# Gated linear attention and a mixture of experts on one core: first unit in halves, rows ahead of weights, verdict in the last expert, the angle's carry placed later

## The chip, the cores and the metric

The kernel runs on one core of one Trainium2 chip. The metric is the device time of one execution in microseconds (us), lower is better. A core has a matrix engine (TensorE, PE in the profile; PEld are its weight loads), three engines for elementwise work (VectorE or DVE, ScalarE or ACT, GpSimd or POOL), and SyncE (SP), which here issues most of the transfers between device memory and on-chip memory. Each engine runs its own list of instructions in order, and waits on semaphores for what others produce. A layer above the kernel's code decides in which order the instructions of one engine stand, so the order of the Python lines is only a wish.

## What is computed

Two blocks follow each other. The first is a linear attention with a complex gate: for each of 4 batches and 8 heads a 48x48 complex state is carried over 768 time steps.

```python
mag = np.sqrt(a_re * a_re + a_im * a_im)
scale = np.minimum(mag, 0.999) / (mag + 1e-06)
a_re_n, a_im_n = (a_re * scale, a_im * scale)
for t in range(S):
    new_re = ar * S_re - ai * S_im
    new_im = ar * S_im + ai * S_re
    kv = np.einsum('bhd,bhe->bhde', k[:, :, t], v[:, :, t])
    S_re, S_im = (new_re + kv, new_im)
    y[:, :, t] = np.einsum('bhd,bhde->bhe', q[:, :, t], S_re)
```

Its output, 3072 rows of 384 numbers, goes into the second block: each row chooses one of 8 experts by the largest of 8 logits, and the expert is two matrix products.

```python
expert_idx = np.argmax(logits, axis=1)
...
h = np.maximum(x_sorted[lo:hi] @ w1[e], 0.0)   # w1[e]: 384 x 1024
y_sorted[lo:hi] = h @ w2[e]                    # w2[e]: 1024 x 384
...
return gate_w[:, None] * y
```

## The kernel before

The attention is computed in chunks of 128 time steps. A *unit* is one such chunk of two batches, a tile of 128 x 768 numbers for each input (128 x 384 a batch); there are 12. The gate is turned into a logarithm of its size, `A`, and an angle, `ai`; both are summed along time by products with triangular matrices (`csl` and `cst`). The chain for a unit alternates between ScalarE and VectorE:

```python
def decay_steps(u):
    ar, ai = T["ar", u], T["ai", u]
    ...
    def s0():
        act(out=A, in_=ar, func=AF.Ln)
    def s1():
        act(out=R, in_=A, func=AF.Exp, scale=-1.0)
        nc.vector.tensor_tensor(out=ai, in0=ai, in1=R, op=OP.mult)
        act(out=R, in_=ai, func=AF.Square)
    def s2():
        act(out=R, in_=R, func=AF.Ln, bias=1.0)
        nc.vector.scalar_tensor_tensor(out=A, in0=A, scalar=2.0, in1=R, ...)
    def s3():
        act(out=R, in_=A, func=AF.Exp, scale=-0.5, bias=ln2e6)
        nc.vector.scalar_tensor_tensor(out=A, in0=A, scalar=LN_CAP2, in1=R, ...)
    return [s0, s1, s2, s3]
```

The angle then goes through an arctangent. From unit 2 on it also needs the angle that the same batches had reached at the end of the chunk before (`fl`); this is the *carry*. The last row is taken out of the tile by a small transfer, added to on VectorE, and put back by another:

```python
def decay_angle(u):
    act(out=th, in_=th, func=AF.Arctan)
    if u * U >= B:
        nc.gpsimd.dma_start(out=T["c0", u], in_=th[0:1]...)      # "c<-ai" in the profile

def carry_angle(u):
    if u * U >= B:
        nc.vector.scalar_tensor_tensor(out=c0, in0=T["fl", u - B // U], ..., in1=c0, ...)
        nc.gpsimd.dma_start(out=T["th", u][0:1]..., in_=c0)      # "ai<-c"
```

Sines and cosines of the summed angle (`CS`) turn the scaled queries and keys (`Q`, `K`), which TensorE transposes (`tp`); copies `qt` and `kt` of the transposed tiles feed the products `at`, and so on to the output `y`. The program starts with the loads, with matmuls on an identity matrix that serve no result (`busy`, tile `idle`; they keep TensorE at work), and with unit 0's chain. In the loop, unit u's sums stand beside unit u+1's chain:

```python
load_a(0)          # ar, ai of unit 0
load_qkv(0)
...                # the gate weights wg
load_a(1)
busy(None, 30)
table("natural_log_exp_and_others")
for f in decay_steps(0):
    f()
...
for u in range(NU + 1):
    ...
        steps = decay_steps(u + 1) if u + 1 < NU else []
        own = [lambda c=c: decay_sums(u, c) for c in range(U)]
        steps = steps[:1] + (own + steps[1:] if u == 0 else own[:1] + steps[1:2] + own[1:] + steps[2:])
        for i, f in enumerate(steps):
            f()
            if i == 1:
                carry_angle(u)
```

After the attention, rows have been scattered to memory in the order of their experts (`xs`). An expert's rows are gathered (`sq`, and `gi` for gate and index), transposed on VectorE (`xt`, function `turn`), multiplied by w1 (`hps`), cut at zero (`ht`), multiplied by w2 (`yps`), scaled by the gate (`y`) and scattered to the output. Expert 0 comes in two parts. Weights have two buffers, rows have two, and SyncE issues all these loads in order.

```python
rest0 = gather(0, FIRST, tiles(CAPS[0] - FIRST))
experts_at(range(1, E), False)
load_w(1)
...
parts = [(0, [P] * (FIRST // P), own0), (0, tiles(CAPS[0] - FIRST), rest0)]
xt = turn(parts[0][1], own0[0])
for e in range(E):
    while parts and parts[0][0] == e:
        sizes, (sq, gi) = parts.pop(0)[1:]
        if not parts and e + 1 < E:
            parts.append((e + 1, tiles(CAPS[e + 1]), gather(e + 1, 0, tiles(CAPS[e + 1]))))
        ...
        def ahead():                   # called between hps and yps
            if parts:
                T["xt"] = turn(parts[0][1], parts[0][2][0])
        expert(sizes, xt, *W_T[e], gi, todo, ahead)
        xt = T["xt"]
    if e + 2 < E:
        load_w(e + 2)
    ...
    if e == E - 2:
        verdict()
```

Beside experts 1 to 6, ScalarE and GpSimd check that the inputs lie in the range for which the fast attention is valid. `verdict` gathers these checks into a flag by a few VectorE operations and one tiny matmul (`bp`); at the very end of the program the flag decides whether a slow attention has to run instead, which does not happen with these inputs.

Of the kernel before, what the change touches and what calls it, by code (L numbers as in the profile page):

```python
# [10 lines left out]
FP = mybir.dt.float32  # L11
# [3 lines left out]
OP = mybir.AluOpType  # L15
# [5 lines left out]
P = 128  # L21
# [16 lines left out]
def kernel(  # L38
# [189 lines left out]
    def act(**kw):  # L228

        ins = nc.scalar.activation(**kw)  # L230
        if "act" in T:
            queue(ins, T["act"])
        T["act"] = ins
# [20 lines left out]
                queue(w, m)  # L254
            m = w

    def load(u, names):
        for nm, src in names:
            if nm == "v":
                t = vbuf[u % 3][:, :, :, 0:D]  # L260
                T[nm, u] = vbuf[u % 3]
            else:
                t = ld.tile([P, U, H, D], FP, tag=nm, name=nm, bufs=3 if nm == "ai" else 2)
                T[nm, u] = t.rearrange("p c h d -> p (c h d)")
            s, b = divmod(u * U, B)
            T["ld"] = nc.sync.dma_start(
                out=t.rearrange("p c h d -> p (c h) d"),
                in_=src[b : b + U, :, s * P : (s + 1) * P, :].rearrange("b h t d -> t (b h) d"),
            )

    def load_a(u):
        load(u, (("ar", a_re), ("ai", a_im)))
# [1 line left out]
    def load_qkv(u):  # L274
        load(u, (("q", q), ("k", k), ("v", v)))

    def decay_steps(u):

        ar, ai = T["ar", u], T["ai", u]
        A = un.tile([P, W], FP, tag="A", name="A")  # L280
        R = un.tile([P, W], FP, tag="R", name="R", bufs=1)
        T["L", u], T["th", u] = A, ai

        def s0():
            act(out=A, in_=ar, func=AF.Ln)

        def s1():
            act(out=R, in_=A, func=AF.Exp, scale=-1.0)
            nc.vector.tensor_tensor(out=ai, in0=ai, in1=R, op=OP.mult)
            act(out=R, in_=ai, func=AF.Square)  # L290

        def s2():
            act(out=R, in_=R, func=AF.Ln, bias=1.0)
            nc.vector.scalar_tensor_tensor(out=A, in0=A, scalar=2.0, in1=R, op0=OP.mult, op1=OP.add)

        def s3():

            act(out=R, in_=A, func=AF.Exp, scale=-0.5, bias=ln2e6)
            nc.vector.scalar_tensor_tensor(out=A, in0=A, scalar=LN_CAP2, in1=R, op0=OP.min, op1=OP.subtract)

        return [s0, s1, s2, s3]

    def decay_angle(u):

# [51 lines left out]
    def angle_sums(u, c):  # L356

        if c == 0:
            for nm in ("f", "fa"):
                T[nm, u] = un.tile([P, W], FP, tag=nm, name=nm, bufs=1)  # L360
        sl = slice(c * DM, (c + 1) * DM)
        f = T["f", u][:, sl]
        cs = sums("cst", u, c)
        m = mm(cs, tri_turn, T["th", u][:, sl])
        if u == 0 and c == 1:
            busy(m, 28)
        r = ch.tile([P, DM], FP, tag="r", name="r")
# [182 lines left out]
    def gather(e, s, sizes):  # L550

        n, w = len(sizes), sum(sizes)
        f, nb = w // P, -(-w // TB)
        sq = gp.tile([P, nb, KD * TB], FP, tag="sq", padded_shape=[P, CAP // TB, KD * TB], name="sq")
        gi = gp.tile([P, n, 2], FP, tag="gi", padded_shape=[P, CT, 2], name="gi", bufs=3)
        rows = xs[0:NS].rearrange("(e s) c -> e s c", s=CAP)[ds(ex[e], 1), s : s + nb * TB]
        for a in range(QB):  # L560
            x = rows[:, :, a * KD * TB : (a + 1) * KD * TB]
            nc.sync.dma_start(out=sq[a * TB : (a + 1) * TB], in_=x.rearrange("o (b j) c -> j (o b) c", j=TB))
        nc.sync.dma_start(out=gi[:, :f], in_=rows[:, : f * P, DM:].rearrange("o (i p) c -> p (o i) c", p=P))
        if f < n:
            nc.sync.dma_start(out=gi[0 : w - f * P, f], in_=rows[:, f * P : w, DM:].rearrange("o p c -> (o p) c"))
        return sq, gi

    load_a(0)
    load_qkv(0)
    for z in range(2):  # L570
        nc.sync.dma_start(
            out=wg[z * DP : z * DP + D, :, 0:E],
            in_=w_gate.rearrange("(i z d) e -> z d i e", z=2, d=D)[z],
        )
    load_a(1)
    busy(None, 30)
    table("natural_log_exp_and_others")
    for f in decay_steps(0):
        f()
    table("trig_and_small")  # L580
    decay_angle(0)
# [5 lines left out]
    for u in range(NU + 1):  # L587
        if 0 < u < NU:
            load_qkv(u)
        for i in range(NS // (P * BL)):  # L590
            if 2 + i * 2 // (NS // (P * BL)) == u:
                blank(i)

        if u < NU:
            steps = decay_steps(u + 1) if u + 1 < NU else []
            own = [lambda c=c: decay_sums(u, c) for c in range(U)]
            steps = steps[:1] + (own + steps[1:] if u == 0 else own[:1] + steps[1:2] + own[1:] + steps[2:])
            table("natural_log_exp_and_others")
            for i, f in enumerate(steps):
                f()  # L600
                if i == 1:
                    carry_angle(u)
            for f in T.pop("chosen", []):
                f()
            for c in range(U):
                angle_sums(u, c)
            table("trig_and_small")
            rotation(u)
            if u + 1 < NU:
                decay_angle(u + 1)  # L610
            if u == NU - 1:
                while T["put"]:
                    place()
                experts_at(range(1), True)
                load_w(0, range(KD + KF // 2))
                own0 = gather(0, 0, [P] * (FIRST // P))
        if u < NU:
            place()
        for f in T.pop("route", []):
            T["put"] += f()  # L620
        for c in range(U):
            g = (u - 1) * U + c
            if g >= 0:
                scores(g)
            if u < NU:
                decayed(u, c)
            if g > 0:
                outputs(g - 1)

            n = {NT - GR: GR, NT - U: U}.get(g)  # L630
            if n:
                if n == GR:
                    queue(table("natural_log_exp_and_others"), T["copied"])
                choose(g - n, n)()
                T["put"] += route(g - n, n)
                while T["put"]:
                    place()
        for _ in range(2 if u >= NU - 2 else 1):
            place()
        if u > 2 and u % 2 and u < NU - 1:  # L640

            j = (u - 3) * U
            T["chosen"] = [choose(j, GR)]
            T["route"] = [lambda j=j: route(j, GR)]
        if u + 2 < NU:
            load_a(u + 2)
# [10 lines left out]
    def tiles(n):  # L657
        return [P] * (n // P) + [n % P] * (n % P > 0)

    rest0 = gather(0, FIRST, tiles(CAPS[0] - FIRST))  # L660
    experts_at(range(1, E), False)
    load_w(1)
    xp = ctx.enter_context(tc.tile_pool(name="xp", bufs=2))
    hp = ctx.enter_context(tc.tile_pool(name="hp", bufs=2))
# [134 lines left out]
        nc.vector.tensor_copy(out=flag, in_=bp)  # L799

    flag = const([1, 2], "flag", I32)
    parts = [(0, [P] * (FIRST // P), own0), (0, tiles(CAPS[0] - FIRST), rest0)]
    xt = turn(parts[0][1], own0[0])
    for e in range(E):
        if e in (1, E - 1):
# [25 lines left out]

    TS = 16
# [85 lines left out]
    def others():  # L918
        with tc.tile_pool(name="mo", bufs=1) as mo:
# [8 lines left out]
            with tc.For_i(0, E, 1) as ev:  # L928
# [8 lines left out]
                with tc.For_i(0, NT, 1) as jv:  # L937
                    nc.vector.tensor_copy(out=fi, in_=fr[:, ds(jv, 1)])
                    xg = gp.tile([P, XW], FP, tag="sq", padded_shape=[P, KD * CAP], name="xg")
                    gi = gp.tile([P, 1, 2], FP, tag="gi", padded_shape=[P, CT, 2], name="gi", bufs=3)  # L940
# [45 lines left out]
```

## Time and profile before

| | |
|---|---|
| time, median of 3 | 563.52 us (563.12 to 565.4) |
| span of the profiled execution | 561.2 us |
| TensorE busy | 530.6 us, 95% |
| VectorE, ScalarE, GpSimd busy | 271.4, 278.0, 130.2 us |
| mean granted TensorE clock | 0.984 |
| attention, about 0 to 283 us; experts, to 555 us | TensorE's holes lie mostly in the first |

The span is a little shorter than the time, as it is that of one execution between its first and last instruction. In the profile, "L81" is the line of the helper that records every matmul, so matmuls are told apart by their tiles. A line such as `csl<-A,tri_half 128x384` names the tile written, the tiles read, and the shape. "[2.93 <-DVE A]" is how long the engine had been idle before an instruction, and who released it. The granted clock is the share of TensorE's full clock that it was given.

### The profile page before, as it was taken

The page shows a single profiled execution, that of the slowest core. Times are in us where ns is not written, and L with a number is a line of the kernel's source. Part 1 is how long each engine was busy: PE and PEld are TensorE (multiplying, and loading weights), DVE is VectorE, ACT ScalarE, POOL GpSimd, SP SyncE. Part 2 cuts the span into 40 slices and gives each one's busy share as a digit, 9 for nine tenths or more (in the row PEclk, how much of TensorE's full clock was granted, in tenths as well). Part 3 has the DMA queues.
Part 4 walks back from the last instruction along what each step waited for, and adds up shares of the span by engine and source line. Part 5 has one row for each costly group of instructions (what it writes and reads, how often), then busy time and mean ns, then how long its engine had stood idle before and what let it go on. Part 6 is the DMA issues. An engine that isn't in the chain of part 4 may idle for free.

```text
span 561.2 us, 8750 instructions
## 1 busy us (share of the span) xinstructions
PE 530.6 (95%) x3294; PEld 367.8 (66%) x3294; DVE 271.4 (48%) x637; ACT 278.0 (50%) x468; POOL 130.2 (23%) x148
## 2 busy tenths in 40 slices
PE   6699999989999999999999899999999999999895
PEld 6587677768778778777776545555555555565462
DVE  2567788688888888878442122112222131210310
ACT  5777967857787687745310105326152341616100
POOL 2101111131141140210221003406143250604201
PEclk9879999989999999999999999999999999999998
DMA  9999995937575543460117893373945718390001
GB/s 158 182 220 260 246 158 66 171 83 119 108 140 95 107 93 58 98 231 12 48 60 234 231 266 127 110 204 130 280 133 178 231 48 263 126 293 15 26 2 42
DMA packets 163534, 79.32 MB, mean 141 GB/s; under 512 B 144864, under 2 KB 156829, under 8 KB 162587
## 3 DMA queue, kind: packets, MB, share of 16 engines
q1 hardware_dynamic: 158619, 69.04, 53.8%
q0 software_dynamic: 4864, 9.63, 5.1%
q8 instruction: 28, 0.46, 0.3%
q14 instruction: 23, 0.19, 0.1%
HBM read 63.30 MB, written 15.46 MB: 140 GB/s over the span
## 4 chain that ended last, share of the span: by engine, by line
PE 73%; ACT 3%; DVE 3%; issue 2%; DMA 2%; POOL 1%; POOLq 0%; DVEq 0%; ACTq 0%
PE hps L81 24%; PE yps L81 21%; PE y L81 7%; PE at L81 6%; PE tp L492 5%; PE dk L81 3%; PE csl L81 2%; PE cst L81 2%; PE tpx L542 2%; DMA c<-ai 2%; PE lt L81 1%; ACT L242 1%; PE lp L81 1%; POOL cai L774 1%; POOL cs L771 1%
## 5 line engine op out<-in xcount | busy, mean ns | idle before, releaser
L81 PE MATMUL hps<-xt,w1t 128*128 128x256 f32 (+8 forms) x432 | 133.9, 469 | 2.3 <-DVE xt L679 2.3
L81 PE MATMUL yps<-w2t,ht 128*128 128x384 f32 (+6 forms) x464 | 135.0, 487 | 0.0
L81 PEld LDWEIGHTS hps<-xt,w1t 128*128 128x128 f32 x432 | 80.0, 190 | 54.3 <-issue 24.8
L81 PEld LDWEIGHTS yps<-w2t,ht 128*128 128x128 f32 (+6 forms) x464 | 75.9, 177 | 57.0 <-issue 7.1
L713 ACT ACTIVATE ht<-hps 128x256 f32<-128x256 f32 (+8 forms) x36 | 17.0, 472 | 132.2 <-PE hps L81 131.3
L730 DVE TENSOR_SCALAR y<-yps,gi 128x384 f32<-128x384 f32 (+2 forms) x24 | 14.8, 616 | 106.6 <-PE yps L81 106.6
L717 DVE TENSOR_SCALAR ht<-hps 128x256 f32<-128x256 f32 (+8 forms) x36 | 19.2, 533 | 83.6 <-PE hps L81 83.5
L81 PE MATMUL at<-qt,kt 96*128 96x128 f32 x384 | 54.9, 284 | 3.4 <-DVE kt L84 2.7
L81 PEld LDWEIGHTS at<-qt,kt 96*128 96x128 f32 x384 | 49.2, 195 | 10.4 <-DVE kt L84 3.2
L81 PE MATMUL y<-am,v 128*64 128x128 f32 x384 | 51.0, 286 | 0.6 <-DVE am L500 0.5
L693 POOL DMA_INDIRECT out_dram<-y,gi x29 | 28.2, 972 | 93.0 <-DVE y L730 42.8
L470 POOL DMA_INDIRECT xs<-x,slot x24 | 26.2, 1090 | 89.2 <-DMA xs<-x,slot 29.1
L81 PE MATMUL y<-qt,G 96*64 96x128 f32 x320 | 46.0, 281 | 0.7 <-DVE G L537 0.7
L771 POOL TENSOR_TENSOR cs<-cs,cw 128x768 f32<-128x768 f32 x12 | 21.7, 1807 | 87.1 <-ACT cw L767 87.1
L500 DVE TENSOR_TENSOR am<-at,tri 128x512 f32<-128x512 f32 x48 | 33.0, 687 | 14.7 <-PE at L81 14.6
L81 PEld LDWEIGHTS y<-am,v 128*64 128x64 f32 x384 | 33.1, 137 | 9.6 <-issue 8.0
L492 PE MATMUL tp<-ident,Q 128*96 128x128 f32 x192 | 33.5, 285 | 2.1 <-DVE Q L398 1.7
L81 PEld LDWEIGHTS y<-qt,G 96*64 96x64 f32 x320 | 32.6, 137 | 4.4 <-issue 2.7
L242 ACT ACT_TABLE_LOAD x27 | 34.6, 1283 | 1.2 <-PEq L972 0.8
L84 ACT COPY qt<-tp 96x512 f32<-96x512 f32 x48 | 27.8, 581 | 14.0 <-PE tp L492 13.9
L81 PEld LDWEIGHTS dk<-v,K 128*96 128x96 f32 x320 | 31.1, 170 | 3.2 <-issue 1.1
L81 PE MATMUL dk<-v,K 128*96 128x48 f32 x320 | 31.7, 252 | 0.8 <-DVE t L530 0.8
(140 smaller groups left out, 745.9 us busy)
## 6 DMA issues: line engine op xcount, KB each, us to landing
w1t<-in_moe_w_dram SPq DMA_DIRECT2D x7, 1536.0 KB, 6.6
w2t<-in_moe_w_dram SPq DMA_DIRECT2D x7, 1536.0 KB, 7.2
xs<-zrow SPq DMA_DIRECT2D x7, 772.0 KB, 8.7
ar<-in_a_re_dram SPq DMA_DIRECT2D x12, 384.0 KB, 5.9
ai<-in_a_im_dram SPq DMA_DIRECT2D x12, 384.0 KB, 6.6
q<-in_q_dram SPq DMA_DIRECT2D x12, 384.0 KB, 5.8
k<-in_k_dram SPq DMA_DIRECT2D x12, 384.0 KB, 6.2
v<-in_v_dram SPq DMA_DIRECT2D x12, 384.0 KB, 5.1
```

What stands on the lines that cost most here:

```text
L81: return nc.tensor.matmul(o, lhsT=lhsT, rhs=rhs, start=start, stop=stop, skip_group_check=True)
L84: (nc.scalar.copy if i % 2 else nc.vector.tensor_copy)(out=o, in_=in_)
L242: ins = nc.scalar.preload_act_table_set(name)
L470: pool(nc.gpsimd.indirect_dma_start(out=xs[:, :], out_offset=bass.IndirectOffsetOnAxis(ap=to[:, i : i + 1], axis=0), in_=x[:, i], in_offse ...
L492: nc.tensor.transpose(out=tp[0:DD, j], in_=X[:, hg * 4 + j], identity=ident)
L500: nc.vector.tensor_tensor(out=am, in0=at, in1=bc(tri, 1, 4), op=OP.mult)
L542: nc.tensor.transpose(out=tp[:, i].rearrange("p z d -> p (z d)"), in_=xt[:, i], identity=ident)
L693: T["out"] = nc.gpsimd.indirect_dma_start(out=out, out_offset=bass.IndirectOffsetOnAxis(ap=idx, axis=0), in_=y[0:m], in_offset=None, bound ...
L713: relu = nc.scalar.activation(out=ht[:, f], in_=ps, func=AF.Relu)
L717: nc.vector.tensor_scalar(out=ht[:, f], in0=ps, scalar1=0.0, scalar2=None, op0=OP.max)
L730: nc.vector.tensor_scalar(out=y[0:m], in0=ps[0:m], scalar1=gate, scalar2=None, op0=OP.mult)
L771: nc.gpsimd.tensor_tensor(out=s, in0=s, in1=w, op=OP.add)
```

## The change

Five things change. (1) Unit 0's loads of ar and ai and its decay chain are cut in two halves (one batch each), whose steps are interleaved so that ScalarE works on one while VectorE works on the other. The square becomes a step of its own. ar of unit 1 is loaded before q and k of unit 0, and ai of unit 1 before v. (2) The filler matmuls are 28 and 38 in place of 30 and 28. (3) The rows of expert 1 are gathered before its weights are loaded, and later experts' rows one expert earlier than they were; `gi` gets a fourth buffer for this. (4) The verdict moves from behind expert 6 to between hps and yps of expert 7, the last. (5) The carry is called after the last step of the next unit's chain, in place of after the second, so that VectorE meets it later.

```diff
-    def load(u, names):
+    def load(u, names, cuts=1):
+        n = U // cuts
+        for c in range(0, U, n):
             ...
-    def decay_steps(u):
+    def decay_steps(u, cuts=1):
             ...                      # s1 split: Square becomes a step of its own
+        w = W // cuts
+        return [steps(slice(i * w, i * w + w)) for i in range(cuts)]
...
         if u == 0 and c == 1:
-            busy(m, 28)
+            busy(m, 38)
...
-        gi = gp.tile([P, n, 2], ..., bufs=3)
+        gi = gp.tile([P, n, 2], ..., bufs=4)
...
-    load_a(0)
-    load_qkv(0)
+    load(0, (("ar", a_re), ("ai", a_im)), 2)
+    load(1, (("ar", a_re),))
+    load(0, (("q", q), ("k", k)))
+    load(1, (("ai", a_im),))
+    load(0, (("v", v),))
...
-    load_a(1)
-    busy(None, 30)
+    busy(None, 28)
-    for f in decay_steps(0):
+    first, second = decay_steps(0, 2)
+    for f in first[:2] + second[:1] + first[2:3] + second[1:2] + first[3:4] + second[2:4] + first[4:] + second[4:]:
         f()
...
-            steps = steps[:1] + (own + steps[1:] if u == 0 else own[:1] + steps[1:2] + own[1:] + steps[2:])
+            if u == 0:
+                steps = steps[:2] + own + steps[2:]
+            else:
+                steps = steps[:1] + own[:1] + steps[1:3] + own[1:] + steps[3:]
             for i, f in enumerate(steps):
                 f()
-                if i == 1:
+                if i == min(4, len(steps) - 1):
                     carry_angle(u)
...
-    rest0 = gather(0, FIRST, tiles(CAPS[0] - FIRST))
+    part(0, FIRST)
     experts_at(range(1, E), False)
+    part(1)
     load_w(1)
...
-            if not parts and e + 1 < E:
-                parts.append((e + 1, tiles(CAPS[e + 1]), gather(e + 1, 0, tiles(CAPS[e + 1]))))
             last = not parts or parts[0][0] > e
+            if last and e + 2 < E:
+                part(e + 2)
             def ahead():
                 if parts:
                     T["xt"] = turn(parts[0][1], parts[0][2][0])
+                else:
+                    verdict()
...
-        if e == E - 2:
-            verdict()
```

More of the change, by code (lines that the diff above doesn't have):

```diff
@@ L255, in busy @@
             m = w
-    def load(u, names):
[L258 to L269, printed above, removed]
+    def load(u, names, cuts=1):
+        s, b = divmod(u * U, B)
+        n = U // cuts
+        for c in range(0, U, n):
+            for nm, src in names:
+                if nm == "v":
+                    T[nm, u] = vbuf[u % 3]
+                elif c == 0:
+                    t = ld.tile([P, U, H, D], FP, tag=nm, name=nm, bufs=3 if nm == "ai" else 2)
+                    T[nm, u] = t.rearrange("p c h d -> p (c h d)")
+                t = vbuf[u % 3][:, :, :, 0:D] if nm == "v" else T[nm, u].rearrange("p (c h d) -> p c h d", h=H, d=D)
+                T["ld"] = nc.sync.dma_start(
+                    out=t[:, c : c + n].rearrange("p c h d -> p (c h) d"),
+                    in_=src[b + c : b + c + n, :, s * P : (s + 1) * P, :].rearrange("b h t d -> t (b h) d"),
+                )
     def load_a(u):
@@ L275, in load_qkv, with steps, s0, s1 @@
         load(u, (("q", q), ("k", k), ("v", v)))
-    def decay_steps(u):
-        ar, ai = T["ar", u], T["ai", u]
+    def decay_steps(u, cuts=1):
         A = un.tile([P, W], FP, tag="A", name="A")
         R = un.tile([P, W], FP, tag="R", name="R", bufs=1)
[L282 to L301, printed above, removed]
+        T["L", u], T["th", u] = A, T["ai", u]
+        def steps(sl):
+            ar, ai, a, r = [t[:, sl] for t in (T["ar", u], T["ai", u], A, R)]
+            def s0():
+                act(out=a, in_=ar, func=AF.Ln)
+            def s1():
+                act(out=r, in_=a, func=AF.Exp, scale=-1.0)
+                nc.vector.tensor_tensor(out=ai, in0=ai, in1=r, op=OP.mult)
+            def s2():
+                act(out=r, in_=ai, func=AF.Square)
+            def s3():
+                act(out=r, in_=r, func=AF.Ln, bias=1.0)
+                nc.vector.scalar_tensor_tensor(out=a, in0=a, scalar=2.0, in1=r, op0=OP.mult, op1=OP.add)
+            def s4():
+                act(out=r, in_=a, func=AF.Exp, scale=-0.5, bias=ln2e6)
+                nc.vector.scalar_tensor_tensor(out=a, in0=a, scalar=LN_CAP2, in1=r, op0=OP.min, op1=OP.subtract)
+            return [s0, s1, s2, s3, s4]
+        w = W // cuts
+        return [steps(slice(i * w, i * w + w)) for i in range(cuts)]
     def decay_angle(u):
@@ L557, in gather @@
         sq = gp.tile([P, nb, KD * TB], FP, tag="sq", padded_shape=[P, CAP // TB, KD * TB], name="sq")
-        gi = gp.tile([P, n, 2], FP, tag="gi", padded_shape=[P, CT, 2], name="gi", bufs=3)
+        gi = gp.tile([P, n, 2], FP, tag="gi", padded_shape=[P, CT, 2], name="gi", bufs=4)
         rows = xs[0:NS].rearrange("(e s) c -> e s c", s=CAP)[ds(ex[e], 1), s : s + nb * TB]
@@ L594 @@
         if u < NU:
-            steps = decay_steps(u + 1) if u + 1 < NU else []
+            steps = decay_steps(u + 1)[0] if u + 1 < NU else []
             own = [lambda c=c: decay_sums(u, c) for c in range(U)]
-            steps = steps[:1] + (own + steps[1:] if u == 0 else own[:1] + steps[1:2] + own[1:] + steps[2:])
+            if u == 0:
+                steps = steps[:2] + own + steps[2:]
+            else:
+                steps = steps[:1] + own[:1] + steps[1:3] + own[1:] + steps[3:]
             table("natural_log_exp_and_others")
@@ L658, in tiles, with part @@
         return [P] * (n // P) + [n % P] * (n % P > 0)
-    rest0 = gather(0, FIRST, tiles(CAPS[0] - FIRST))
+    parts = [(0, [P] * (FIRST // P), own0)]
+    def part(e, s=0):
+        sizes = tiles(CAPS[e] - s)
+        parts.append((e, sizes, gather(e, s, sizes)))
+    part(0, FIRST)
     experts_at(range(1, E), False)
+    part(1)
     load_w(1)
@@ L801 @@
     flag = const([1, 2], "flag", I32)
-    parts = [(0, [P] * (FIRST // P), own0), (0, tiles(CAPS[0] - FIRST), rest0)]
     xt = turn(parts[0][1], own0[0])
@@ L939, in others @@
                     xg = gp.tile([P, XW], FP, tag="sq", padded_shape=[P, KD * CAP], name="xg")
-                    gi = gp.tile([P, 1, 2], FP, tag="gi", padded_shape=[P, CT, 2], name="gi", bufs=3)
+                    gi = gp.tile([P, 1, 2], FP, tag="gi", padded_shape=[P, CT, 2], name="gi", bufs=4)
                     nc.gpsimd.indirect_dma_start(
```

## The prediction

> **What bounds the kernel now.** I read the page's first two parts, then TensorE's list of waits, then the timeline around each long wait, and last a table of 2 us stretches for the granted clock.
>
> ```profile
> PE 530.6 (95%) x3294; PEld 367.8 (66%) x3294; DVE 271.4 (48%) x637; ACT 278.0 (50%) x468; POOL 130.2 (23%) x148
> ...
> PE   6699999989999999999999899999999999999895
> ...
> PEclk9879999989999999999999999999999999999998
> ```
>
> TensorE is busy 95% of the span, and the others half of it or less. So only two things can shorten the run: TensorE's holes (561.2 - 530.6 = 30.6 us) and the stretches in which its clock is low. The digits show both: slices 1, 2 and 9 of the busy row, and slices 2, 3 and 9 of the clock row. The list of TensorE's waits names the holes:
>
> ```profile
> PE csl L81 <- DVE A L299: 5.9, 2, 2.9
> PE at L81 <- DVE kt L84: 2.7, 2, 2.4
> PE hps L81 <- DVE xt L679: 2.3, 1, 2.3
> PE bp L81 <- DVE two L796: 2.3, 1, 2.3
> ...
> PE tp L492 <- DVE Q L398: 1.7, 2, 1.4
> ```
>
> The columns are total, times, longest. Two waits are for the decay chain of units 0 and 1 (A), one of 2.4 is at a copy of transposed keys (kt), one at the rows of expert 1 (xt), one at the verdict (bp). The timeline of the start (start, duration, engine, line, operation, and in brackets the idle time before it) shows the cost of the first two:
>
> ```profile
> 12.80 1.56 PE L81 MATMUL csl<-A,tri_half 128*128 128x384 f32 x4 [2.93 <-DVE A L299]
> ...
> 15.98 0.84 ACT L230 ACTIVATE A<-ar 128x768 f32<-128x768 f32 x1 [0.77 <-DMA ar<-in_a_re_dram]
> ...
> 24.83 1.54 PE L81 MATMUL csl<-A,tri_half 128*128 128x384 f32 x2 [2.93 <-DVE A L299]
> 25.10 0.94 ACT L230 ACTIVATE CS<-fa,mhalfpi 128x768 f32<-128x768 f32 x1
> ...
> 27.81 1.09 PE L492 MATMUL tp<-ident,Q 128*96 128x128 f32 x4 [1.44 <-DVE Q L398]
> ```
>
> Useful work (the first tp) begins at 27.81. Between the end of the filler matmuls (21.89) and there TensorE does two csl matmuls and nothing else. The table of 2 us stretches (stretch, length, busy time of PE, PEld, DVE, ACT, POOL, then the granted clock) shows what this sets off:
>
> ```profile
> 22.00:24.00 2.00, 0.00 (x0) 0.00 (x0) 1.00 (x2) 1.13 (x2) 0.00 (x0) 1.00 1.07 187
> 24.00:26.00 2.00, 1.17 (x2) 0.40 (x2) 0.77 (x1) 1.99 (x3) 0.00 (x0) 0.74 0.99 181
> 26.00:28.00 2.00, 0.56 (x2) 0.19 (x2) 1.20 (x2) 1.98 (x4) 0.00 (x0) 0.50 1.19 193
> ...
> 32.00:34.00 2.00, 2.00 (x8) 1.24 (x8) 1.16 (x2) 0.00 (x0) 0.00 (x0) 0.50 1.03 181
> 34.00:36.00 2.00, 2.00 (x14) 2.00 (x13) 0.23 (x1) 1.58 (x3) 0.00 (x0) 0.70 1.01 185
> 36.00:38.00 2.00, 2.00 (x24) 1.95 (x24) 1.85 (x4) 2.00 (x6) 1.14 (x2) 1.00 1.13 182
> ```
>
> The clock is 0.50 from about 25 to 35.4, and in 32 to 34 ScalarE is idle behind a slow TensorE. The same happens on a small scale at unit 5: VectorE's carry waits 3.92 us for its DMA, the copy kt behind it is late, TensorE idles 2.38 us, and the clock is 0.50 from about 117 to 120.3.
>
> ```profile
> 112.63 0.16 DVE L315 SCALAR_TENSOR_TENSOR c<-fl,c 96x8 f32<-96x8 f32 x1 [3.92 <-DMA c<-ai]
> ...
> 116.25 0.94 PE L81 MATMUL at<-qt,kt 96*128 96x128 f32 x6 [2.38 <-DVE kt L84]
> ```
>
> **What the Trainium skill says.** "TensorE: Matmul & The Clock Gate", Part 1, states that TensorE's clock is halved after an idle window of about 3.4 us and restored after about as much sustained work, and that the window runs free. The trace agrees in kind (0.50 some 3 us after the filler ended) and shows a longer way back: busy from 27.8, restored at 35.4. The same page, "Architectural detail: the array is 16× 32×32, not 1× 128×128", says that VectorE and ScalarE are strict first in, first out; the 3.92 us before the carry, with kt standing behind it, are that. "ScalarE: Activation LUTs", "What ACT_TABLE_LOAD costs", gives about 1283 ns a load; the trace has 1283 ns, 27 times. The change neither adds nor removes one.
>
> **The change part by part.** *Unit 0 in halves, and loads reordered.* A 128x768 operation takes 0.84 us on ScalarE and 0.96 on VectorE, a 128x384 one 0.47 and 0.55, so halves cost little and let the two engines overlap. Loads of 384 KB land about 2.1 us apart (ar at 4.9, ai at 7.05, the sixth at 15.95 with the small gate loads between). Halves should then land at about 3.9, 5.0, 6.0, 7.05, ar of unit 1 at 9.1 in place of 15.95, q 11.2, k 13.3, ai of unit 1 15.4. Followed along ScalarE's new order: Ln a 3.9, Exp a 4.4, Ln b 6.0, Square a 6.4, Exp b 6.8, Ln a 7.15, Square b 7.9, Ln b 8.4, Exp a 8.8, Exp b 9.6 (VectorE first does five small setup operations), ended at 10.1. The last A is ready at 10.75, before 12.75; arctan at 11.4, before 13.07. Ln of unit 1 starts at 13.55, before 15.98, and waits for no DMA. Its product with ai starts at 15.4 (the landing), VectorE's six operations behind it end at 19.1, STT 20.05, Exp 21.0, table load 22.3, so the sines (CS) start near 22.35, before 25.10. The same 2.71 us from CS to the first tp give 25.1. Gain: 27.8 - 25.1 = **2.7 us**.
>
> *The filler of 28 matmuls becomes 38.* 28 of them took 6.41 us, so 38 take 8.7. Started behind cst at about 13.8 they end at 22.5, when A of unit 1 is just ready (22.0). What is left idle is from 23.3 to 25.1, in place of 2.93 and 1.44 us with one matmul between. I expect the clock to stay at 1.00. The work of 27.81 to 35.4, 7.6 us at half speed, would need 3.8 at full; VectorE and ScalarE are then nearer to the bound (in 28 to 50 they are busy 15.5 and 16.5 of 22 us), so I count **3.3**.
>
> *Rows of expert 1 ahead of its weights.* The four sq loads stood behind the weights in SyncE's queue (7.60 us for their issue alone), and VectorE's program had the transposes behind the last addition of the tile before, which ended at 322.1. In the changed program they stand before that addition and after a product that ended at 318.85; the first takes 0.75, so it is done at 319.6, and TensorE is free at 320.9. Gain **2.3**. The weights are issued some 5 us later than 299.6, need about 7 us to land and are wanted at 320.9. Later experts' rows also come an expert earlier; they had no wait to lose.
>
> *Verdict in the last expert.* bp stands between hps and yps of the last expert in place of before hps. Its inputs were ready at 524.4, some 15 us before that place comes. hps can start at about 522.2. Gain **2.3**.
>
> *The carry.* In VectorE's built order it moves little: for unit 5 the carry still stands behind the same product K, and its DMA still stands behind the same scatter on GpSimd. But the copy kt stands two operations earlier behind it (ai*R 0.87 and Qe 0.47 now follow kt), so the hole of 2.38 shrinks by some 1.2 and the half-clock stretch (3.2 us, worth 1.6) may go. I count **1.5**. The waits for other units (1.26, 1.51, 1.90, 1.08, 0.93) hardly touch TensorE.
>
> Sum: 2.7 + 3.3 + 2.3 + 2.3 + 1.5 = 12.1. The whole attention part has a new order of instructions and its small holes (about 7 us beside the ones named) are drawn anew, with less slack on VectorE and ScalarE; I take off 1.4. That is 10.7, and 563.5 - 10.7 = **552.8 us**.
>
> **The rivals.** (1) *The clock falls anyway.* The window runs free; with 1.8 us idle and thin work from 25 to 30 it may still catch one. For it: at unit 5 a hole of 2.38 was enough. Against: 2.93 us idle at 9.87 did not lower the clock. Time: 556. (2) *Loads bind the start.* DMA engines are full from 2 to 36 us (share 0.99 or more in every 2 us stretch), so loads that come earlier push q, k and v back; if ai of unit 1 lands at 17 and not 15.4, the chain loses 1.6. Time: 554.5. (3) *The gain at the start is given back by units 1 to 4*, where VectorE and ScalarE are busy 48.0 and 50.9 of 63 us and the carry waits for a DMA of 4 us whatever comes before it. Against: TensorE is at 59.5 of 63 there, so it sets the pace. Time: 558, the experts' 4.6 being left. (4) *More than I count*: if the second unit's sines come at 39 (before 46.15), the start alone is worth 7, and unit 5 loses both hole and slow clock: 549.
>
> **Range and chances.** The experts' 4.6 are the surest; the start's 6.0 may be 3 to 7.5; the carry's 1.5 may be -1 to 4. The low end takes the good ends (549.5), the high end only half of the start and nothing of the carry (557). Faster by 2% means under 552.25, just below my number, so it is nearly even: 0.42; within 2% 0.56; slower 0.02.
>
> **What would show it right or wrong.** Right: first tp at about 25 us; clock at 1.00 through 24 to 36; sines of unit 1 near 40; no wait at the first hps of expert 1 nor at bp; hps of the last expert following yps at once; a hole of about 1 us at unit 5. Wrong: ScalarE or VectorE waiting for ai of unit 1 beyond 16; 0.50 in the clock row after 22; new holes of over 1 us from 50 to 280, above all at kt or cst behind the carry; hps of expert 1 waiting for w1t.

## The result

The changed kernel takes 556.68 us (median of 4 runs, 555.56 to 558.93), the kernel before 563.32 (4 runs): ratio 0.9884, 95% interval 0.984 to 0.9928. That is 6.6 us of the predicted 10.7, and 1.2% of the time: it falls under "within 2%", which had been given the larger chance, 0.56. The first two parts of the page of the changed kernel (busy time; then TensorE's busy row and clock row in 40 slices):

```profile
PE 536.2 (97%) x3310; PEld 371.5 (67%) x3310; DVE 271.3 (49%) x640; ACT 279.4 (50%) x473; POOL 132.1 (24%) x148
...
PE   8799999999999999989999999999999999999995
...
PEclk9979999999999999989999999999999999999999
```

The holes shrank from 30.6 to 18.4 us (554.6 - 536.2), 12.2 less, but the span only by 6.6: TensorE is busy 5.6 us longer, with 8 more filler matmuls and with work at a low clock. Slice 9 is mended in both rows; slice 3 (28 to 42 us) still has a low clock; slice 18 (236 to 250 us) is new, with a hole and a low clock. The list of TensorE's waits in the changed kernel (total, times, longest) says who is behind them:

```profile
PE cst L81 <- issue: 2.2, 1, 2.2
PE tpx L554 <- ACT xt L551: 2.1, 3, 0.7
PE tp L504 <- DVE Q L410: 1.8, 1, 1.8
...
PE csl L81 <- ACT Ei L230: 1.1, 1, 1.1
...
PE tp L504 <- DVE kt L84: 0.9, 2, 0.5
```

The waits at hps (2.3), at bp (2.3) and for the decay chain A (5.9) are gone; that at kt fell from 2.7 to 0.9. New is the cst of the last unit. The timeline of the start (start, duration, engine, line, operation, idle time before it in brackets):

```profile
10.65 1.46 PE L81 MATMUL csl<-A,tri_half 128*128 128x384 f32 x4
...
24.80 0.64 PE L504 MATMUL tp<-ident,Q 128*96 128x128 f32 x4 [1.76 <-DVE Q L410]
...
27.45 1.24 PE L81 MATMUL csl<-A,tri_half 128*128 128x384 f32 x2 [1.14 <-ACT Ei L230]
...
42.11 0.94 ACT L230 ACTIVATE CS<-fa,mhalfpi 128x768 f32<-128x768 f32 x1
```

The first tp stands at 24.80 (27.81 before), as predicted. But a second hole of 1.14 follows, and the table of 2 us stretches (stretch, length, busy time of PE, PEld, DVE, ACT, POOL, then granted clock, DMA share, GB/s) shows that the clock fell all the same:

```profile
22.00:24.00 2.00, 1.04 (x4) 0.31 (x3) 0.29 (x2) 1.99 (x4) 0.00 (x0) 1.00 1.33 214
24.00:26.00 2.00, 0.98 (x7) 0.73 (x8) 2.00 (x3) 1.97 (x3) 0.00 (x0) 1.00 1.47 168
26.00:28.00 2.00, 0.86 (x5) 0.47 (x4) 2.00 (x4) 2.00 (x4) 0.00 (x0) 0.97 1.40 212
28.00:30.00 2.00, 2.00 (x12) 1.64 (x11) 1.75 (x3) 1.28 (x3) 0.00 (x0) 0.50 1.31 207
...
34.00:36.00 2.00, 2.00 (x14) 1.13 (x13) 0.79 (x2) 1.68 (x4) 0.00 (x0) 0.82 1.28 208
```

From 22 to 28 TensorE works 2.88 of 6 us, in pieces; 0.50 begins at 28 and lasts until about 35. The unit's sines come at 42.11, 4 us ahead of 46.15, but not near 40.

The last unit's timeline in the changed kernel:

```profile
233.01 1.45 SPq L212 DMA_DIRECT2D w1t<-in_moe_w_dram  x3
234.25 2.95 POOL L482 DMA_INDIRECT xs<-x,slot  x1 [1.18 <-DMA xs<-x,slot]
234.64 2.08 SPq L212 DMA_DIRECT2D w2t<-in_moe_w_dram  x4
235.29 0.16 DVE L327 SCALAR_TENSOR_TENSOR c<-fl,c 96x8 f32<-96x8 f32 x1
237.20 0.54 POOL L330 DMA_DIRECT2D ai<-c  x1
...
243.02 1.62 PE L81 MATMUL cst<-ai,tri_turn 128*128 128x384 f32 x2 [2.20 <-issue]
```

The carry is ready at 235.45, but a scatter holds GpSimd until 237.20, and only then does the carry's transfer back (ai<-c) start. Expert 0's weights (w1t, w2t) were put into the queue at 233 to 237. The transfer of 3 KB takes 5.7 us to land, by the list of transfers, so it is in at 242.9 and cst starts at 243.02. The page calls this wait "issue"; the time of landing shows what it was. The 2 us stretches around it:

```profile
238.00:240.00 2.00, 2.00 (x21) 1.82 (x20) 1.71 (x4) 1.92 (x4) 0.00 (x0) 1.00 1.02 355
240.00:242.00 2.00, 0.82 (x13) 0.58 (x12) 0.84 (x2) 0.87 (x2) 0.00 (x0) 1.00 1.05 397
242.00:244.00 2.00, 0.98 (x2) 0.71 (x3) 0.00 (x0) 0.00 (x0) 0.68 (x1) 0.73 0.83 301
244.00:246.00 2.00, 2.00 (x9) 1.69 (x9) 1.16 (x4) 0.00 (x0) 0.33 (x1) 0.50 0.28 108
```

The weights fill the DMA engines (share 1.0, up to 397 GB/s), all compute engines run dry, and the clock falls to 0.50 behind the hole. Before, the same cst stood here:

```profile
243.39 0.88 PE L81 MATMUL cst<-ai,tri_turn 128*128 128x384 f32 x2 [0.92 <-issue]
```

It had 0.92 us of idle time ahead of it and no low clock after it, although its transfer back, issued at 238.24, took 5.1 us as well. TensorE then had other work until 242.5, in the changed kernel only until 240.8.

The questions: what are the experts' parts and the start parts worth by themselves; is the last unit's loss due to the weights; does a longer filling keep the clock. A fourth came from the first answers: why attention ends earlier even where none of its instructions moved.

### The profile page after: what moved, and what is told of

It reads as the page before. It is cut to its first block, busy times and chain, and to the rows that moved or that the text cites. A ratio compares the mean times of both kernels' runs of the same rounds, so it can differ in the third digit from the quotient of the medians.

```text
span 554.6 us, 8781 instructions
## 1 busy us (share of the span) xinstructions
PE 536.2 (97%) x3310; PEld 371.5 (67%) x3310; DVE 271.3 (49%) x640; ACT 279.4 (50%) x473; POOL 132.1 (24%) x148
## 4 chain that ended last, share of the span: by engine, by line
PE 84%; ACT 4%; issue 4%; DVE 3%; DMA 3%; POOL 0%; SPq 0%; POOLq 0%; DVEq 0%; ACTq 0%
PE yps L81 24%; PE hps L81 24%; PE y L81 8%; PE at L81 7%; PE tp L504 7%; PE dk L81 4%; PE cst L81 3%; PE csl L81 2%; DMA c<-ai 2%; PE tpx L554 2%; PE lt L81 1%; ACT L242 1%; ACT R L230 1%; DMA ar<-in_a_re_dram 1%; ACT xt L551 1%
## 5 line engine op out<-in xcount | busy, mean ns | idle before, releaser
L482 POOL DMA_INDIRECT xs<-x,slot x24 | 28.2, 1173 | 90.1 <-DMA xs<-x,slot 32.0
L81 PEld LDWEIGHTS y<-am,v 128*64 128x64 f32 x384 | 31.5, 136 | 10.5 <-issue 7.5
L504 PE MATMUL tp<-ident,Q 128*96 128x128 f32 x192 | 32.2, 282 | 2.7 <-DVE Q L410 1.8
L81 PEld LDWEIGHTS y<-qt,G 96*64 96x64 f32 x320 | 30.8, 136 | 4.8 <-issue 3.8
```

The source lines that it names most:

```text
L81: return nc.tensor.matmul(o, lhsT=lhsT, rhs=rhs, start=start, stop=stop, skip_group_check=True)
L482: pool(nc.gpsimd.indirect_dma_start(out=xs[:, :], out_offset=bass.IndirectOffsetOnAxis(ap=to[:, i : i + 1], axis=0), in_=x[:, i], in_offse ...
L504: nc.tensor.transpose(out=tp[0:DD, j], in_=X[:, hg * 4 + j], identity=ident)
```

## The experiments

All twelve were timed in rounds beside the kernel before, on four occasions, and each ratio is to the kernel before of the same occasion. "us" is the difference of the ratio from 1, times 563.3; a difference of two rows is uncertain by some 3 us.

| kernel | median us | ratio (95%) | us |
|---|---|---|---|
| changed | 556.68 | 0.9884 (0.984 to 0.9928) | -6.5 |
| e1_start | 570.30 | 1.0128 (1.0087 to 1.0168) | +7.2 |
| e2_experts | 553.03 | 0.9803 (0.9767 to 0.9839) | -11.1 |
| e4_weights_late | 552.31 | 0.9801 (0.9767 to 0.9835) | -11.2 |
| e5_fill44 | 551.25 | 0.9775 (0.9743 to 0.9808) | -12.7 |
| e6_gi4 | 558.33 | 0.9904 (0.9868 to 0.994) | -5.4 |
| e7_gi5 | 562.28 | 0.9978 (0.9958 to 0.9999) | -1.2 |
| e8_pad | 559.66 | 0.9927 (0.9901 to 0.9953) | -4.1 |
| e9_best | 547.76 | 0.9708 (0.9666 to 0.975) | -16.4 |
| e10_start4 | 563.17 | 0.9991 (0.9967 to 1.0016) | -0.5 |
| e11_late | 553.49 | 0.9821 (0.979 to 0.9851) | -10.1 |
| e12_nostart | 554.63 | 0.9872 (0.9841 to 0.9903) | -7.2 |
| e13_fill38 | 551.05 | 0.9797 (0.9765 to 0.9828) | -11.4 |

### The parts by themselves

**e1_start**: the kernel before, with parts (1) and (2) alone.

```diff
+    load(0, (("ar", a_re), ("ai", a_im)), 2)
+    first, second = decay_steps(0, 2)
-            busy(m, 28)
+            busy(m, 38)
```

> The kernel before with the start alone (unit 0 in halves, loads reordered, square as its own step, fillers 28 and 38); experts and verdict as before. Theory (the start's lead is real but is given back at the last unit, where the carry's transfer back stands behind the weights of expert 0): first tp at about 24.8 us, lead of 4 to 6 us near 130 us, a hole of about 2 us at cst near 243, lead at the first expert below 2 us; so 561.5 us or a ratio of 0.996. Rival (the lead survives and the experts' parts are worth less than their holes): 559 or less, ratio 0.992.

It is slower than the kernel before, which neither outcome had foreseen, though the first tp stands at 25.29. In the trace a hole at kt takes the start's gain back at once:

```profile
52.49 0.53 PE L504 MATMUL tp<-ident,Q 128*96 128x128 f32 x3 [2.17 <-DVE kt L84]
```

The traced run was the fastest of six (563.3 us); what the others, at 568.8 to 573.2, lose besides, it cannot show. Their mean clock was 0.975 to 0.981 in place of 0.985, so a part of it is time at low clock; where, is not recorded.

**e2_experts**: parts (3) and (4) alone, with the fourth buffer for `gi`.

```diff
+    part(0, FIRST)
     experts_at(range(1, E), False)
+    part(1)
     load_w(1)
+                else:
+                    verdict()
```

> The kernel before with rows of expert 1 ahead of its weights and the verdict in the last expert alone. Theory: both holes of 2.3 us go and nothing else changes: 558.8 us, ratio 0.992. Rival (later weights of expert 1 or the verdict between hps and yps bring new holes): 560.5 or more.

Faster by 11.1 us where the experts' two holes hold 4.6 and 558.8 us was expected. In the trace the holes are gone, and the rest is in attention, which ends 5.1 us earlier although TensorE's and VectorE's instructions stand there in the old order: the first tp comes at 26.34, and the hole of unit 5 is 0.94.

### The last unit and the filling

**e4_weights_late**: the changed kernel, with expert 0's weights queued on SyncE behind the gather of its rows. `queue` sets an instruction behind another in the program.

```diff
-                load_w(0, range(KD + KF // 2))
                 own0 = gather(0, 0, [P] * (FIRST // P))
+                load_w(0, range(KD + KF // 2))
-                queue(nc.sync.dma_start(out=o[:, i], in_=x[:, i]), T["ld"])
+                queue(nc.sync.dma_start(out=o[:, i], in_=x[:, i]), T["g"])
```

> The changed kernel with the load of expert 0's weights put behind the gather of its rows in SyncE's queue (it then starts near 251 us in place of 233). Theory (the last carry's transfer back takes 5.7 us because it stands behind these weights): it lands in under 3 us, the hole of 2.2 us at cst near 243 and the half clock behind it go, and the time falls by 2 to 4 us against the changed kernel, to about 553.5; expert 0's first hps does not wait, as the weights land near 260. Rival 1 (the transfer is slow for another reason, the 2.95 us scatter on GpSimd before it): hole above 1.2 us, time 556. Rival 2 (the weights come too late): a wait at the first hps of expert 0.

The ratio falls by 0.0083, 4.7 us. Its timeline at the same place:

```profile
236.39 0.55 POOL L330 DMA_DIRECT2D ai<-c  x1
...
239.94 0.91 PE L81 MATMUL cst<-ai,tri_turn 128*128 128x384 f32 x2
...
247.78 2.48 SPq L212 DMA_DIRECT2D w1t<-in_moe_w_dram  x3
```

The transfer back is still issued behind the scatter, but lands in 1.9 us in place of 5.7; hole and low clock are gone, and hps does not wait for the weights. In attention the two programs have the same order on every compute engine, so the traffic of the weights was what made the transfer slow.

The late issue behind the scatter has its share in the hole too. e1_start has the same order in attention and the weights at their old place, but in its trace no scatter stood in the way: the carry was ready at 240.54, ai<-c was issued at 241.12 and took 5.5 us to land, and the cst came after 0.76 us:

```profile
246.68 0.88 PE L81 MATMUL cst<-ai,tri_turn 128*128 128x384 f32 x2 [0.76 <-ACT qt L84]
```

(The page names the copy qt, which had ended at 245.98; the landing near 246.6 came later.) In the changed kernel the issue came 1.75 us after the carry in place of 0.58. By this estimate 1.2 of the 2.20 us belong to the late issue; a landing in 1.9 us hides it, as e4_weights_late shows.

**e5_fill44**: the changed kernel with 44 filling matmuls.

```diff
-            busy(m, 38)
+            busy(m, 44)
```

> The changed kernel with 44 filler matmuls in place of 38 behind cst of unit 0, so that less of 22 to 25 us is idle. Theory (the clock fell because of the idle pieces from 22.1 to 28): idle before the first tp falls from 1.76 to about 0.4 us; if this is enough the clock stays at 1.00 from 28 to 35, sines of unit 1 come at 40 in place of 42.1, yet the time falls by only 0 to 2 us, as the last unit takes the lead back. If the remaining 1.1 us before csl is enough to lower the clock, nothing changes: ratio to the changed kernel 1.000. Rival (the start was the whole loss): 3 us less.

Faster than the changed kernel by 6.1 us, where 0 to 2 were expected, but this one number changed the built order of the whole attention, so the gain is not the filling's alone. (The last unit's hole is 1.4 us in this order, and is followed by no low clock.) What the filling was meant for is seen in its stretches:

```profile
22.00:24.00 2.00, 2.00 (x15) 1.38 (x13) 0.42 (x1) 2.00 (x3) 0.00 (x0) 1.00 1.36 217
24.00:26.00 2.00, 1.18 (x8) 0.78 (x8) 2.00 (x3) 1.97 (x3) 0.00 (x0) 1.00 1.47 167
26.00:28.00 2.00, 0.86 (x4) 0.46 (x3) 2.00 (x4) 2.00 (x5) 0.00 (x0) 1.00 1.37 212
28.00:30.00 2.00, 2.00 (x23) 2.00 (x22) 1.55 (x3) 0.81 (x2) 0.00 (x0) 1.00 1.28 215
```

22 to 24 is full, and the clock stays at 1.00 through the start. It falls later: in a new hole at kt it drops, and is 0.50 until about 54; this run as a whole had a mean clock of 0.992.

```profile
47.96 0.88 PE L504 MATMUL tp<-ident,Q 128*96 128x128 f32 x3 [2.24 <-DVE kt L84]
```

### The address

With three buffers for `gi`, the tiles ar, ai, q and k begin at byte 105,888 and so on of each partition, 32 past a multiple of 64; the fourth buffer of 32 bytes moves them to 105,920, a multiple of 64. Every kernel above that gained in attention had the fourth buffer, and e1_start did not. Three runs vary this and nothing else.

**e6_gi4**: the kernel before with the fourth buffer. No instruction of a compute engine moves; SyncE has a few waits less in the experts' part.

```diff
-        gi = gp.tile([P, n, 2], ..., bufs=3)
+        gi = gp.tile([P, n, 2], ..., bufs=4)
```

> The kernel before, with a fourth buffer for the index tile and nothing else. The buffer is 32 bytes per partition, so every tile that is allotted after it moves by 32 bytes, and the tiles ar, ai, q and k then begin at a multiple of 64 bytes. Theory (the address makes the loads faster): about 558 us (555.5 to 560.5), the loads from 2 to 36 us at 195 to 215 GB/s where the kernel before had 174 to 190, the hole at the first matmul of unit 5 under 1.2 us where it was 2.38; the two holes of the experts stay. Rival (the fourth buffer is only there for the fewer waits, and the gain in attention comes from the moved rows and verdict): 563.4 us, same rates, same hole.

**e7_gi5**: the changed kernel with `bufs=5`; same order, old alignment.

> The changed kernel, with five buffers for the index tile where it has four: ar, ai, q and k again begin 32 bytes past a multiple of 64. Same instructions in the same order. Theory (address): 5 us or more slower than the changed kernel, 561 to 566 us, loads at 172 to 190 GB/s in the first 36 us, first transform matmul later than 24.8 us. Rival (address is of no account): 556.7 us, 195 to 213 GB/s.

**e8_pad**: the kernel before with 32 unused bytes ahead of all large tiles, so that v, the weights and the zero rows are shifted too. No engine's list differs, not even in its waits.

```diff
+    const([P, 8], "pad")
```

> The kernel before, with 32 unused bytes per partition ahead of all large tiles: these, the values v, the weights and the scratch tiles too, begin at a multiple of 64 bytes. No instruction differs. Theory (address): as with the fourth index buffer or a little better, 555 to 558.5 us, the loads at 195 GB/s or more. Rival: 563.4 us.

The transfers from 2 to 36 us in the kernel before (packets, bytes, mean rate, packets by size):

```profile
DMA packets 33013, 6.23 MB, mean 183 GB/s; under 512 B 33008, under 2 KB 33012, under 8 KB 33012
```

the same line of e6_gi4:

```profile
DMA packets 35868, 7.17 MB, mean 211 GB/s; under 512 B 35570, under 2 KB 35867, under 8 KB 35867
```

of e7_gi5:

```profile
DMA packets 33015, 6.22 MB, mean 183 GB/s; under 512 B 33006, under 2 KB 33014, under 8 KB 33014
```

and of e8_pad:

```profile
DMA packets 36366, 7.90 MB, mean 232 GB/s; under 512 B 35595, under 2 KB 36365, under 8 KB 36365
```

The changed kernel has 204. So 32 bytes make the same loads 15% faster (211 against 183), another 32 in the changed kernel take it back, and shifting v and the others as well brings 27%. In time e6_gi4 wins 5.4 us and e7_gi5 loses 5.3 against the changed kernel, both as the theory of the address had expected: the address, not the buffer. The tiles on which the engines compute move too, but their work takes the same time: between 40 and 110 us the products am take 687 ns and the copies qt 581 ns in the kernel before and in e6_gi4 alike. e8_pad loads fastest but wins no more than e6_gi4 (4.1 against 5.4, within the uncertainty, and 559.66 us where at most 558.5 was expected; single runs from 556.3 to 563.4). Its traced run, 562.07 us, has a hole of 1.60 us at cst at 57.33 and a low clock behind it that e6_gi4 lacks; so no further gain from the loads beyond 211 GB/s was seen in this order. The hole of unit 5 in e6_gi4:

```profile
112.18 0.94 PE L81 MATMUL at<-qt,kt 96*128 96x128 f32 x6 [1.16 <-DVE kt L84]
```

It was 2.38, and no instruction was moved.

### Together

**e10_start4**: e1_start with the fourth buffer, to be read against e6_gi4.

> The kernel before with the start parts (halves, order of the loads, filling matmuls) and the fourth index buffer, without the experts' parts. It stands against the kernel before with the fourth buffer alone, which took 558.3 us. If the start parts are a loss of their own that the address only shifts: the start parts alone cost 6.9 us at the old address, so about 562 to 566 us. If they are about worth nothing and lost at the old address through the slow loads: 556 to 560 us. If they bring what the prediction gave them: 552.3 to 555 us.

4.9 us slower than e6_gi4, so a loss of their own, the first of the outcomes named. Its waits name the place (the other two are the experts', which it keeps):

```profile
PE cst L81 <- issue: 3.3, 1, 3.3
PE hps L81 <- DVE xt L698: 2.3, 1, 2.3
PE bp L81 <- DVE two L815: 2.3, 1, 2.3
```

It is the last unit's hole again, now 3.3 us where e6_gi4 has 1.44, with a mean clock of 0.57 from 244 to 252 us behind it. At the new address the hole near 50 us shrinks to 0.56; the start parts' loss is then mostly the last unit's.

**e11_late**: e2_experts with late weights; same edit as in e4_weights_late.

> The experts' parts and the fourth index buffer without the start parts (553.0 us), and expert 0's weights behind the gather of its rows. In the trace of the version without late weights the last unit has no large hole. Theory (the weights hurt only where the carry's transfer back is issued late, which the changed order does): 552 to 554 us, no gain. Rival (weights in the middle of attention cost everywhere): 549 to 551 us.

No gain (-10.1 against -11.1): in the old order that cst waited only 0.92 us. The weights hurt only together with the new order. So the start parts without this loss are worth what e4_weights_late has over e11_late: 1.1 us, not told apart from nothing.

**e9_best**: the changed kernel with late weights, 44 filling matmuls, the pad, and `bufs=5` (all large tiles at a multiple of 64).

> The changed kernel with three things added: the weights of expert 0 queued behind the gather of its rows, 44 filling matmuls in place of 38, and 32 bytes of padding together with a fifth index buffer so that all large tiles begin at a multiple of 64 bytes. If the gains of the late weights (4.4 us) and of the start stand side by side: 547 to 551 us. If the order that the longer filling brings gives back in the units what the start gains, as it did with the filling alone: 551 to 553 us.

547.76 us, the fastest of all, 2.9% under the kernel before.

**e12_nostart**: the same without the start parts.

> The best version (547.8 us) without the start parts: experts' parts, late weights, all large tiles at a multiple of 64 bytes. If the start parts, with filling that holds the clock, are worth what their trace shows (first transform 1.5 us or more earlier, clock at full speed): 550 to 553 us. If all of the last gain came from the addresses: 547 to 549 us.

**e13_fill38**: e9_best with 38 filling matmuls; its order is that of e4_weights_late.

> The best version (547.8 us) with the changed kernel's 38 filling matmuls in place of 44; the instruction order is then that of the version with late weights alone (552.3 us), and against that one only the addresses differ. If the longer filling, with the order that it brings, is what makes the start parts pay: 551 to 553 us. If the addresses of the remaining tiles do it: 547 to 549 us.

e12_nostart is slower than e9_best by 9.2 us (6.9 by the medians) and slower than any outcome that had been named, e13_fill38 by 5.0 (3.3 by the medians). Not all of the 9.2 belongs to the start parts: e12_nostart is e11_late at other addresses, and 2.9 us slower than it, about the uncertainty of a difference; its runs fall into two at 550.4 and six from 554.4 to 556.8, and the traced one is among the two. Against e11_late e9_best wins 6.3. So the start parts pay in earnest only with the longer filling and the order that comes with it, and, it seems, with the weights late: e5_fill44, without the latter, is but 1.6 us ahead of e2_experts. Whether filling or order does more was not separated. The remaining addresses alone do nothing more in the new order: e13_fill38 and e4_weights_late differ by 0.2 us. The clock speaks for the filling together with its order: the mean over a run reached 0.998 or 0.999 in 4 of the 6 runs of e9_best, and 0.999 or more in 3 of 6 of e5_fill44, while the changed kernel had 0.982 to 0.993 and e13_fill38 0.986 to 0.996.

**The carry** by itself was not run: the changed kernel with the call at its old place is built to the same instructions in the same order with the same waits on every engine, and so is the kernel before with only this call moved. So there is nothing to time.

## Why the prediction came out as it did

The time lies in the range by luck. With the same instructions and the tiles 32 bytes further on it is 562.28 us (e7_gi5), above the 557 of the high end; what brought it to 556.68 was the address, which no term of the sum had. Foreseen were 4.6 for the experts and 2.7 + 3.3 + 1.5 - 1.4 = 6.1 for attention. Measured, from kernel to kernel: experts' parts -5.7 (e2_experts against e6_gi4), address -5.4 (e6_gi4), start parts with the carry +4.6 (the changed kernel against e2_experts). That is -6.5. The changes to attention lost 4.6 where 6.1 was to be won, and the address nearly cancels this. Two of the prediction's own signs of being wrong came: 0.50 in the clock row after 22, and a new hole of over 1 us at cst behind the carry.

- **Rows of expert 1 and verdict, 2.3 + 2.3: right.** Both waits are gone from the list, the 4.6 us agree with -5.7 within its uncertainty, and hps did not wait for the later weights.
- **Start, 2.7: right in the trace.** The first tp came 3.0 earlier. The start parts alone, at the old addresses, bring 2.5 of this (25.29 in e1_start), the faster loads alone 1.3 (26.47 in e6_gi4); the two do not add up.
- **Clock, 3.3: this step failed.** "I expect the clock to stay at 1.00" overlooked the holes behind the first tp (0.23 and 1.14): the stretch of thin work is 6 us long, not 1.8. Rival 1 named this. With 44 matmuls the mean clock is 0.998 or more in 7 of the 12 runs of e5_fill44 and e9_best. These runs are 1.6 us faster than the others of the same kernel (medians 550.71 against 552.34, and 547.2 against 548.9), which is an estimate of what the clock is worth there: half of the 3.3.
- **Carry, 1.5: right about unit 5, wrong about what moves it.** The call's place changes no instruction. The new order in attention comes with the start parts, and it does what was foreseen: at unit 5 the copy kt stands ahead of ai*R and Qe, and the hole shrinks from 2.38 to 1.20 at old addresses (e7_gi5) with no low clock behind it. The address alone brings it to 1.16, both together to 0.50. What this is worth in time by itself was not measured. In e7_gi5:

```profile
115.04 0.61 PE L504 MATMUL tp<-ident,Q 128*96 128x128 f32 x4 [1.20 <-DVE kt L84]
```

and in the changed kernel

```profile
110.71 0.61 PE L504 MATMUL tp<-ident,Q 128*96 128x128 f32 x4 [0.50 <-DVE kt L84]
```

- **New order, -1.4: mis-sized.** The last unit alone costs 4.7 (e4_weights_late). It is rival 3 in kind, the start's gain given back, but in the changed kernel not in units 1 to 4: it comes in the unit where the weights start. In other kernels these units do give back: a hole at kt near 50 us of 2.17 in e1_start, 3.18 in e7_gi5, both at old addresses, and 2.24 in e5_fill44.
- **Missing: the address, -5.4.** The fourth buffer was read as a matter of waits alone.
- **Rival 2** (loads bind) did not come in the changed kernel: VectorE's product with ai of unit 1 starts at 15.18, with 15.4 foreseen, and waited for ScalarE; no wait on TensorE names a transfer of ar or ai. At old addresses it came in part: in e7_gi5 the same product waits for its transfer until 15.78, and the first tp stands at 25.39. **Rival 4**: sines at 42.11, not 39.
- **Range.** Its ends do not quite follow from its terms: the good ends give 4.6 + 7.5 + 4 - 1.4 = 14.7, so 548.8 and not 549.5, and the bad ones 4.6 + 3.0 - 1.4 = 6.2, so 557.3 and not 557.

What stays open: why the new order leaves TensorE less other work in the last unit; what opens and closes the hole at kt near 50 us; and why e1_start scatters up to 573, and e8_pad and e12_nostart between two times.

## What to carry to other kernels

When a part wins time in a stage whose instructions it does not touch, compare the addresses of the tiles before looking for a subtle reason, and test with some bytes of padding. A small transfer on the critical path should not share the DMA engines with prefetched weights: look where the prefetch starts, and let it start after the last such transfer. A gain at the start is only as good as the place where the new order puts its next hole, so time each part alone.

## What the runs showed of the hardware

Loads of 192-byte rows depend on where they land on chip: 183 GB/s from 2 to 36 us with all at an odd multiple of 32 bytes, 204 to 211 with ar, ai, q and k at a multiple of 64, 223 to 232 with v too. The Trainium skill, "DMA: Bandwidth & Descriptors", section "How a descriptor splits into AXI transactions", says that a transaction starts at a multiple of 256 bytes, and that a descriptor which begins between two such places pays 32-byte beats from the one below. An estimate from that page, if it holds for the writing side as well: of four rows one behind the other, from a start that is 160 past a multiple of 256 (105,888), the last bytes lie at 352, 288, 224 and 416, which is 11 + 9 + 7 + 13 = 40 beats; from 192 past (105,920) it is 12 + 10 + 8 + 6 = 36. A row of v, one every 256 bytes, pays 13 beats at its old place, 224 past, and 6 with the pad. Four rows each of ar, ai, q, k and v then need 212 beats before, 196 with the fourth buffer and 168 with the pad, so 8% and 26% more rate; measured were 15% and 27%. 105,952 (e7_gi5) gives 40 again, as its 183 GB/s does; 105,984, a multiple of 256, gives 36 again, and e12_nostart, which has it, loads at 230 GB/s where e8_pad loads at 232. So the direction agrees everywhere and the size for the pad; the 15% is more than the estimate, and that this is the mechanism was not shown.

A transfer of 3 KB took 5.7 us to land beside 355 to 397 GB/s of weights (5.0 to 6.9 in the other traces that have the weights there and show its landing), and 1.9 and 1.7 without them (e4_weights_late, e11_late).

The clock is not settled by the length of the holes alone. The same stretches in e9_best, to be read beside those of e5_fill44:

```profile
24.00:26.00 2.00, 1.17 (x9) 0.78 (x8) 2.00 (x3) 1.97 (x3) 0.00 (x0) 1.00 1.15 232
26.00:28.00 2.00, 0.86 (x4) 0.50 (x2) 2.00 (x4) 2.00 (x5) 0.00 (x0) 0.77 1.19 240
28.00:30.00 2.00, 2.00 (x10) 1.46 (x9) 1.68 (x3) 0.81 (x3) 0.00 (x0) 0.50 1.21 225
```

With the same 44 filling matmuls and the same holes after them (0.60, 0.23 and 1.14 us in both) it stayed at 1.00 in the one trace and went to 0.50 at about 27 in the other. This agrees with the Trainium skill, "TensorE: Matmul & The Clock Gate", Part 1, which says that the window runs free.
